# The opening of a fused attention and FFN kernel: w_out in row parts, Q and K in parts behind w3, a new hand-written order

## The chip, the cores and the metric

The kernel runs on one core of a Trainium2 chip. The metric is the device time of one execution in microseconds (us), lower is better. Its engines are named as in the profile: PE (TensorE matmuls; PEld its weight loads), DVE (VectorE), ACT (ScalarE), POOL (GpSimd) and SP (SyncE, here only DMA issues). Each engine takes its instructions in the order of the program and waits on semaphores for the others.

## The reference

Sliding-window causal attention, window 64, over 8 batches, 8 heads, 576 positions, head size 64; then a multiplicative FFN without a nonlinearity on its 4608 rows of 512:

```python
scores = (q @ k.T) / sqrt(64), kept where 0 <= i - j < 64
x = softmax(scores) @ v                 # heads side by side: 4608 x 512
out = (((x @ w1) * (x @ w2)) @ w3) @ w_out   # w1, w2: 512x1024, w3: 1024x1024, w_out: 1024x512
```

Inputs and output are float32; the kernel computes in float16 with float32 sums.

## The kernel before

**Folding.** Since nothing stands between w3 and w_out, the kernel first makes wc = w3 @ w_out (1024 x 512), in eight blocks of 128 rows (fc = 0 to 7). For each block `fold_t` transposes the 128 x 1024 rows of w3 on PE (eight 128 x 128 transposes into one PSUM bank, then one copy to `w3T`), and `fold_mm` multiplies them by w_out, held in `wo16`, and copies the sum from PSUM to `wc_sb`. Blocks 0 to 3 are done in two column halves of 256, blocks 4 to 7 at once, since w_out comes in two column halves.

**Attention.** Each batch has three query segments of 192 positions. `scores(n)` (n = 3 * batch + segment) computes transposed scores of all eight heads into two PSUM tiles; `weigh(d)` (d = 2n, 2n+1, one for each tile, four heads) is the Exp on ACT and the window mask, either two or four selects on POOL or one multiplication by a 0/1 band on DVE; `values(d)` multiplies by V and by ones (giving the row sums), then Ln and Exp(-x) on ACT and a multiplication on DVE write four heads of 192 rows into `xT`. `keep_sums` sends the logarithms of the sums to a buffer for a range check at the end. Q and K arrive as float16 and are transposed on DVE in blocks (`transposes`, L225), a head parity (hh) at a time. In V's tile the columns between the heads are ones (`ones_of`), and `copy_v` copies rows that two key blocks share.

**FFN.** Rows go in nine groups of 512. `ffn_ab(g, fc)` computes a block of 128 columns of x @ w1 and x @ w2 (16 matmuls into two PSUM banks), ACT copies a, DVE multiplies it by b into `ab`. The form `ffn_ab(g, fc, 2, lo, hi)` does two blocks for 256 of the rows, with twice as many matmuls of half the width. `ffn_o(g, t)` multiplies 128 rows by wc (eight matmuls), copies, and `store` sends them out on SP.

**Memory that sets the order.** PSUM is two pools: `ps_a` has two tiles of two banks (scores and values take them in turn), `ps_f` four banks for everything else, handed out in turn: an allocation waits until the fourth one before it has been read. `w3T` has four buffers.

**Order.** The schedule is manual: every engine runs its instructions in the order in which the functions are called. All loads convert float32 to float16 and are issued on POOL, in between POOL's selects. They use eight semaphores in turn, so POOL waits at a load until the eighth load before it has landed. The opening, up to `tick(24)`, which begins with `scores(6)`, is written out by hand; from there on `tick` and a list of due times set the order. It begins: K and Q of batch 0, w_out half 0, w3 rows 0 to 255, the bands, w3 rows 256 to 511, w_out half 1, w3 rows 512 to 767, three blocks of V. Meanwhile `keep_busy(120)` runs matmuls on an identity matrix, whose result is not used, on PE. Then

```python
    scores(0)
    keep_busy(30)
    fold_t(0)
    fold_t(1)
    scores(1)
```

and so on through the fold, with `values(0)` to `values(5)` among its last blocks, then all eight `ffn_ab(0, fc)`, `scores(3)`, `ffn_o(0, 0)`.

Of the kernel before, what the change touches and what calls it, by code (L numbers as in the profile page):

```python
# [15 lines left out]
P = 128  # L16
# [128 lines left out]
def kernel(  # L145
# [25 lines left out]
    EARLY = 2  # L171
# [30 lines left out]
    def load_qk(b, which, *hhs):  # L202
        src = k if which == "k" else q
        r = RUN[b]
        if (which, b) not in t16s:
            t16s[which, b] = sb.tile([P, 2, TI * D], FP16, name=which + "16", bufs=2)
        t = t16s[which, b]
        if not hhs:
            for j in range(NJ):
                nc.gpsimd.dma_start(  # L210
                    out=t[32 * j:32 * j + 32].rearrange("p hh (i n) -> p (hh i) n", n=r * D),
                    in_=src[b, 2 * j:2 * j + 2].rearrange("hh (i p r) d -> p (hh i) (r d)", p=32, r=r))
        for hh in hhs:
            for i in range(2):
                nc.gpsimd.dma_start(
                    out=t[:, hh, i * r * D:(i + 1) * r * D],
                    in_=src[b, hh:H:2, i * 32 * r:(i + 1) * 32 * r].rearrange("j (p r) d -> j p (r d)", p=32, r=r))

    def transposes(b, which, hh):

        dst = kTs if which == "k" else qTs
        r = RUN[b]
        if hh == 0:
            dst[b] = sb.tile([P, 2, S, 2], FP16, name=which + "T")
        nc.vector.transpose(  # L225
            dst[b][:, hh].rearrange("q t c -> q (t c)").bitcast(I32).rearrange("q (i p r) -> q i r p", p=32, r=r),
            t16s[which, b][:, hh].bitcast(I32).rearrange("p (i r e) -> p i r e", r=r, e=32))
# [44 lines left out]
    def scores(n, now=True):  # L272
# [19 lines left out]
        weigh(2 * n)  # L292
        if now:
            weigh(2 * n + 1)

    def weigh(d):

        s_ps = held.pop(d)
        si = d // 2 % 3
        w = s_ps.shape[-1]  # L300

        pt = sb.tile([P, 2, 2, 256], FP16, name="pt", bufs=6)
        nc.scalar.activation(pt[:, :, :, 0:w], s_ps, AF.Exp, bias=-SHIFT, scale=scale)  # L303

        rows = pt.rearrange("k j a n -> k (j a) n")
        if d % 2 == 1 and d < 6 * EARLY:
            band = bands[min(si, 1)]
            nc.vector.tensor_tensor(rows[:, :, 0:w], rows[:, :, 0:w],  # L308
                                    band[:, 0:w].unsqueeze(1).broadcast_to([P, 4, w]), ALU.mult)
        else:  # L310
            select(rows, si)
        probs[d] = pt

    def values(d):
# [7 lines left out]
        o_ps = ps_a.tile([P, 2, 512], FP32, name="a_ps")  # L322
        if jp == 0:
            lns[b, si] = sb.tile([P, NJ, 192], FP32, name="ln_s", bufs=4)
        y = lns[b, si][:, j0:j0 + 2]
        r = sb.tile([P, 2, 192], FP32, name="r")
        x0 = (b * S + q_base) % RING
        xs = xT[:, j0:j0 + 2, x0:x0 + 192]
        if b < SHORT:
# [12 lines left out]
            o, total = (o_ps[:, e, 0:384].rearrange("p (j n) -> p j n", j=2) for e in range(2))  # L342
            nc.scalar.activation(y, total, AF.Ln)
            nc.scalar.activation(r, y, AF.Exp, scale=-1.0)  # L344
            nc.vector.tensor_tensor(xs, o, r, ALU.mult)  # L345
            return
        for jj in range(2):
            first = True
            for a in range(2):
                c0 = 0  # L350
                for bi, (k0, q0, n, _) in enumerate(seg):
# [6 lines left out]
                    c0 += n  # L358
        nc.scalar.activation(y[0:D], o_ps[D:P, :, 0:192], AF.Ln)  # L359
# [23 lines left out]
    def tick(u):  # L383
# [3 lines left out]
        if m == 0 and n < NS:  # L387
            scores(n, now=False)
        if m == 1 and n < NS:
            weigh(2 * n + 1)  # L390
        if m in (1, 2) and 6 < n <= NS:
            values(2 * n - 3 + m)
        for e in late.get(r, []):
            event(b, *e)
# [59 lines left out]
    def load_w12(i, half):  # L454
        cols = slice(half * 512, half * 512 + 512)
# [3 lines left out]
    def load_wo(half):  # L459
        cols = slice(half * 256, half * 256 + 256)  # L460
        nc.gpsimd.dma_start(out=wo16[:, :, cols], in_=moe_w_out[:, cols].rearrange("(e p) m -> p e m", p=P))  # L461

    def load_w3(n):
        fc = 2 * n
        dst = w3a[:, 2 * fc:2 * fc + 4, :].rearrange("p (f a) n -> p f (a n)", f=2) if n < 2 else \
            xT[:, fc - 4:fc - 2, 2 * S:2 * S + DF]
        nc.gpsimd.dma_start(out=dst, in_=moe_w3[fc * P:fc * P + 2 * P].rearrange("(f p) n -> p f n", p=P))

    def fold_t(fc):
# [6 lines left out]
        dve_cp(w3Ts[fc], tp)  # L476

    def fold_mm(fc, c0, c1, cp):
        o_ps = ps_f.tile([P, DM], FP32, name="f_ps")
        for ec in range(8):  # L480
            nc.tensor.matmul(o_ps[:, c0:c1], w3Ts[fc][:, ec, :], wo16[:, ec, c0:c1], start=(ec == 0), stop=(ec == 7))  # L481
        cp(wc_sb[:, fc, c0:c1], o_ps[:, c0:c1])
# [33 lines left out]
    load_qk(0, "k")  # L516
    make_identity(nc, ident16)
    load_qk(0, "q")
    load_wo(0)
    load_w3(0)  # L520
    make_bands()
    load_w3(1)
    load_wo(1)
    load_w3(2)
    load_v(0, 0, 2, 3)
    for i in range(2):
        ones_of(i, nc.vector)
    for which in "kq":
        for hh in range(2):
            transposes(0, which, hh)  # L530
    keep_busy(120)
    scores(0)
    keep_busy(30)
    fold_t(0)
    fold_t(1)
    scores(1)
    load_w3(3)
    load_v(0, 4, 5)
    fold_mm(0, 0, 256, act_cp)
    fold_mm(1, 0, 256, act_cp)  # L540
    fold_t(2)
    fold_t(3)
    scores(2)
    for i in range(2):
        load_w12(i, 0)
    fold_mm(2, 0, 256, act_cp)
    fold_mm(3, 0, 256, act_cp)
    fold_mm(0, 256, DM, act_cp)
    fold_mm(1, 256, DM, act_cp)
    fold_t(4)  # L550
    fold_t(5)
    fold_mm(2, 256, DM, act_cp)
    fold_mm(3, 256, DM, act_cp)
    copy_v(0, 1)
    fold_mm(4, 0, DM, act_cp)
    values(0)
    values(1)
    fold_t(6)
    fold_mm(5, 0, DM, act_cp)
    values(2)  # L560
    values(3)
    copy_v(0, 4)
    fold_t(7)
    fold_mm(6, 0, DM, act_cp)
    values(4)
    values(5)
    fold_mm(7, 0, DM, act_cp)
    for i in range(2):
        load_w12(i, 1)
    load_qk(1, "k")  # L570
    load_qk(1, "q")
    load_v(1, 0, 2, 3, 4, 5)
    for n in range(3):
        keep_sums(n)
    for fc in range(8):
        ffn_ab(0, fc)
        if 2 <= fc < 6:
            transposes(1, "kkqq"[fc - 2], fc % 2)
    load_qk(2, "k")
    load_qk(2, "q")  # L580
    copy_v(1, 1)
    copy_v(1, 4)
    scores(3)
    ffn_o(0, 0)
    store()
    scores(4)
    load_v(2, 0, 2, 3)
    ffn_o(0, 1)
    store()
    scores(5)  # L590
    transposes(2, "k", 0)
    ffn_o(0, 2, act_cp)
    store()
    values(6)
    transposes(2, "k", 1)
    values(7)
    load_v(2, 4, 5)
    ffn_o(0, 3)
    store()
    values(8)  # L600
    transposes(2, "q", 0)
    values(9)
    load_qk(3, "k")
    load_qk(3, "q")
    ffn_ab(1, 0, 2, 0, 256)
    values(10)
    transposes(2, "q", 1)
    ffn_ab(1, 2, 2, 0, 256)
    values(11)
    for n in range(3, 6):  # L610
        keep_sums(n)
# [75 lines left out]
```

## Time and profile before

| | |
|---|---|
| median of 3 runs | 268.28 us (267.68 to 268.68) |
| profiled execution | 268.59 us, of which the span from the first to the last of the program's instructions is 266.8 us |
| PE busy | 254.4 us of the span (95%) |
| DVE, ACT, POOL busy | 169.7, 151.4, 178.7 us |
| granted TensorE clock | 0.997 |
| first `fold_t` on PE | 17.43 us |
| first `ffn_ab` on PE | 39.94 us |
| `scores(6)`, the first step of `tick(24)`, on PE | 72.87 us |

The profile has a page of totals; a timeline and a chain of waits give starts and durations in us from the start of the span. A row such as "17.43 1.07 PE f_ps L474 x16" says: from 17.43 us on, 1.07 us, 16 instructions of line 474 on PE that write the tile f_ps. DMA rows give the bytes that are written (float16) and the median time from issue to landing.

### The profile page before, as it was taken

To read this page: it belongs to the slowest core of one execution; us is meant where nothing else is said; L and a number is where in the kernel's file an instruction comes from. 1 tells how busy PE (TensorE), PEld (TensorE's weight loads), DVE (VectorE), ACT (ScalarE), POOL (GpSimd) and SP (SyncE) were. 2 spreads that over 40 slices of the span, in tenths; PEclk is the share of its full clock that TensorE was granted. 3 is DMA by queue.
4 is the path that set the end of the run, shared out by engine and by line. 5 is a ranking of instruction groups with operands and counts; after the bars stand their busy time and mean duration, and the time that the engine had idled before them with its cause. 6 is when DMAs were issued, how large, how long until landed. Compare 5 with 4: busy or idle time off the path is not lost.

```text
span 266.8 us, 6600 instructions
## 1 busy us (share of the span) xinstructions
PE 254.4 (95%) x2608; PEld 149.7 (56%) x2608; DVE 169.7 (64%) x260; ACT 151.4 (57%) x261; POOL 178.7 (67%) x243
## 2 busy tenths in 40 slices
PE   3979999998999999999999999999999999999992
PEld 3968654445886445545556984545455445444441
DVE  6644454978775675986687567668786565564531
ACT  1037474367656577758874855777498748342300
POOL 7979826679879999999898739687766345005000
PEclk9999999999999999999999999999999999999998
DMA  5999999999999999899999765998540040012013
GB/s 81 170 207 186 189 207 201 131 181 138 149 106 62 131 206 77 61 165 162 62 106 180 102 43 64 202 105 57 99 96 4 7 150 6 0 53 108 0 57 109
DMA packets 75380, 29.45 MB, mean 110 GB/s; under 512 B 62369, under 2 KB 69793, under 8 KB 75345
## 3 DMA queue, kind: packets, MB, share of 16 engines
q0 software_dynamic: 69920, 19.41, 74.9%
q1 hardware_dynamic: 5280, 9.46, 10.0%
q8 instruction: 21, 0.34, 0.6%
q14 instruction: 15, 0.11, 0.2%
q10 hardware_dynamic: 144, 0.13, 0.1%
HBM read 38.80 MB, written 9.44 MB: 181 GB/s over the span
## 4 chain that ended last, share of the span: by engine, by line
PE 87%; DMA 4%; POOL 2%; DVE 2%; ACT 2%; issue 1%; POOLq 0%; DVEq 0%
PE f_ps L417 48%; PE f_ps L435 22%; PE a_ps L353 5%; PE a_ps L286 4%; PE f_ps L481 4%; DMA ab<-in_moe_w_dram 4%; PE a_ps L337 3%; ACT pt L303 1%; PE f_ps L474 1%; POOL q L210 1%; POOL k L210 1%; DVE xT L345 1%; DVE kT L225 1%; POOL ab L461 0%; DVE pt L308 0%
## 5 line engine op out<-in xcount | busy, mean ns | idle before, releaser
L417 PE MATMUL f_ps<-xT,w_sb 128*128 128x512 f16 (+1 forms) x704 | 131.5, 341 | 0.0
L417 PEld LDWEIGHTS <-w_sb 128*128 128x128 f16 x704 | 66.3, 98 | 50.7 <-issue 0.2
L423 DVE TENSOR_TENSOR ab<-f_ps,a_sb 128x512 f16<-128x512 f32 x72 | 49.6, 689 | 33.0 <-PE f_ps L417 31.2
L303 ACT ACTIVATE pt<-a_ps 128x1024 f16<-128x1024 f32 (+1 forms) x48 | 44.5, 953 | 45.4 <-PE a_ps L286 45.4
L258 POOL TENSOR_SCALAR_AFFINE_SELECT pt<-pt 128x1024 f16<-128x1024 f16 (+2 forms) x56 | 46.1, 824 | 30.6 <-ACT pt L303 30.5
L435 PE MATMUL f_ps<-wc_sb,ab 128*128 128x512 f16 (+1 forms) x296 | 66.4, 374 | 0.0
L422 ACT COPY a_sb<-f_ps 128x512 f32<-128x512 f32 x72 | 41.8, 581 | 36.9 <-PE f_ps L417 36.4
L260 POOL TENSOR_SCALAR_AFFINE_SELECT pt<-pt 128x1024 f16<-128x1024 f16 (+2 forms) x56 | 46.5, 831 | 3.9
L435 PEld LDWEIGHTS <-ab 128*128 128x128 f16 x296 | 27.3, 98 | 28.8
L238 POOL DMA_DIRECT2D v<-in_v_dram x40 | 34.0, 860 | 1.0 <-issue 0.4
L362 DVE TENSOR_TENSOR xT<-a_ps,r 64x384 f16<-64x384 f32 x30 | 16.5, 550 | 22.0 <-ACT r L361 22.0
L437 DVE COPY t2k<-f_ps 128x512 f32<-128x512 f32 (+1 forms) x35 | 23.7, 679 | 8.4 <-PE f_ps L435 7.9
L210 POOL DMA_DIRECT2D q<-in_q_dram x32 | 19.7, 621 | 11.8 <-DMA w_sb<-in_moe_w_dram 8.3
L210 POOL DMA_DIRECT2D k<-in_k_dram x32 | 20.1, 634 | 1.6 <-POOLq L671 1.0
L353 PEld LDWEIGHTS <-v 128*128 128x128 f16 x240 | 15.1, 98 | 6.4
L345 DVE TENSOR_TENSOR xT<-a_ps,r 128x384 f16<-128x384 f32 x18 | 10.0, 553 | 13.0 <-ACT r L344 13.0
L359 ACT ACTIVATE ln_s<-a_ps 64x384 f32<-64x384 f32 x30 | 14.6, 487 | 5.8 <-PE a_ps L353 5.0
L353 PE MATMUL a_ps<-pt,v 128*128 128x128 f16 x240 | 17.2, 215 | 0.0
L363 DVE TENSOR_TENSOR xT<-a_ps,r 64x384 f16<-64x384 f32 x30 | 16.8, 561 | 0.4
L286 PEld LDWEIGHTS <-kT 32*128 32x128 f16 x768 | 10.9, 92 | 9.6 <-issue 9.3
L361 ACT ACTIVATE r<-ln_s 128x384 f32<-128x384 f32 x30 | 15.7, 523 | 1.0
L225 DVE STREAM_TRANSPOSE qT<-q 128x576 int32<-128x576 int32 x16 | 14.7, 928 | 1.6 <-DMA q<-in_q_dram 1.6
(44 smaller groups left out, 184.9 us busy)
## 6 DMA issues: line engine op xcount, KB each, us to landing
out_dram<-t2k SPq DMA_DIRECT2D x35, 256.0 KB
k<-in_k_dram POOLq DMA_DIRECT2D x32, 144.0 KB, 6.3
q<-in_q_dram POOLq DMA_DIRECT2D x32, 144.0 KB, 5.8
v<-in_v_dram POOLq DMA_DIRECT2D x32, 128.0 KB, 5.0
w_sb<-in_moe_w_dram POOLq DMA_DIRECT2D x4, 512.0 KB, 9.7
ab<-in_moe_w_out_dram POOLq DMA_DIRECT2D x2, 512.0 KB, 9.5
ab<-in_moe_w_dram POOLq DMA_DIRECT2D x2, 512.0 KB, 9.4
xT<-in_moe_w_dram POOLq DMA_DIRECT2D x2, 512.0 KB, 10.4
```

The source lines that it names most:

```text
L210: nc.gpsimd.dma_start(out=t[32 * j:32 * j + 32].rearrange("p hh (i n) -> p (hh i) n", n=r * D), in_=src[b, 2 * j:2 * j + 2].rearrange("hh ...
L238: nc.gpsimd.dma_start(out=vh[lo:P, c], in_=v[b, :, s0:s0 + P - lo, :].rearrange("h s d -> s h d"))
L258: nc.gpsimd.affine_select(out=sl, in_=sl, pattern=pat, compare_op=ALU.is_ge, fill=0.0, base=off, channel_multiplier=-1)
L260: nc.gpsimd.affine_select(out=sl, in_=sl, pattern=[[-s, m] for s, m in pat], compare_op=ALU.is_ge, fill=0.0, base=63 - off, channel_multip ...
L286: nc.tensor.matmul(s_ps[j // 2][:, j % 2, o0:o0 + m], kT[part, a, k0:k0 + P, c], qT[part, a, q0:q0 + m, c], start=(c == 0), stop=(c == 1), ...
L303: nc.scalar.activation(pt[:, :, :, 0:w], s_ps, AF.Exp, bias=-SHIFT, scale=scale)
L353: nc.tensor.matmul(o_ps[:, jj, o0:o0 + n], v16[:, si * 2 + bi, j0 + jj, a * D:a * D + P], pt[:, jj, a, c0:c0 + n], start=first, stop=(bi = ...
L417: nc.tensor.matmul(d[:, f * n + c0:f * n + c1], w[:, dc, (fc + f) * P:(fc + f + 1) * P], xT[:, dc, xc:xc + c1 - c0], start=first, stop=(dc ...
L422: act_cp(a_sb[:, 0:nf * n], a_ps[:, 0:nf * n])
L423: nc.vector.tensor_tensor(ab[:, fc:fc + nf, lo:hi], b_ps[:, 0:nf * n].rearrange("p (f n) -> p f n", f=nf), a_sb[:, 0:nf * n].rearrange("p ...
L435: nc.tensor.matmul(o_ps[:, 0:c1 - c0], ab[:, fc, t * P:t * P + P], wc_sb[:, fc, c0:c1], start=(fc == 0), stop=(fc == 7))
L437: cp(o_sb[:, c0:c1], o_ps[:, 0:c1 - c0])
```

## The change

- w_out is loaded in two row parts (rows 0 to 511, 512 to 1023) instead of column halves. Every block's fold is then two calls: `fold_mm(fc, 0)` adds four matmuls of 512 columns into a PSUM bank, which is held until `fold_mm(fc, 1)` adds the other four and copies the sum.
- w3 is loaded first, rows 256 to 511 ahead of all, rows 0 to 127 and 128 to 255 one by one, the rest in pairs of blocks. Q and K of batch 0 come behind it, in eight parts: a part is one head parity (hh) and one half of the positions (i, 288 rows) for all four head pairs, where a load before was two heads with all positions. `transposes` takes a part, and halves are transposed one by one.
- `weigh` is told its engine, and `values` is split: `norm` (Ln, Exp, multiplication) is a call of its own. `tick` calls them in the same places as before.
- The call list of the opening is new. The fold begins before attention; group 0 of the FFN is done mostly in the two-block form; V's blocks, the masks' engines, the copies' engines and the loads stand in other places. One `ones_of` moves to POOL. `keep_busy` runs 115 + 20 + 20 matmuls instead of 120 + 30.

The helpers, cut to what changes:

```diff
+    def part_of(b, which, hh, i):
+        r = RUN[b]
+        src = k if which == "k" else q
+        return src[b, hh:H:2, i * 32 * r:(i + 1) * 32 * r].rearrange("j (p r) d -> j p (r d)", p=32, r=r)
+    def load_part(b, which, hh, i):
+        n = RUN[b] * D
+        nc.gpsimd.dma_start(out=t16_of(b, which)[:, hh, i * n:(i + 1) * n], in_=part_of(b, which, hh, i))
-    def transposes(b, which, hh):
+    def transposes(b, which, hh, *i):
...
+        part = slice(i[0], i[0] + 1) if i else slice(0, TI // r)
...
-    def scores(n, now=True):
+    def scores(n):
...
-        weigh(2 * n)
-        if now:
-            weigh(2 * n + 1)
-
-    def weigh(d):
+
+    def weigh(d, engine=nc.gpsimd):
...
-        if d % 2 == 1 and d < 6 * EARLY:
+        if engine is nc.vector:
...
-        o_ps = ps_a.tile([P, 2, 512], FP32, name="a_ps")
+        opened[d] = o_ps = ps_a.tile([P, 2, 512], FP32, name="a_ps")
...
+    def norm(d):
...
+            nc.scalar.activation(y, total, AF.Ln)
+            nc.scalar.activation(r, y, AF.Exp, scale=-1.0)
+            nc.vector.tensor_tensor(xs, o, r, ALU.mult)
...
-    def load_w12(i, half):
-        cols = slice(half * 512, half * 512 + 512)
+    def load_w12(i, c0, c1):
+        cols = slice(c0, c1)
...
-    def load_wo(half):
-        cols = slice(half * 256, half * 256 + 256)
-        nc.gpsimd.dma_start(out=wo16[:, :, cols], in_=moe_w_out[:, cols].rearrange("(e p) m -> p e m", p=P))
+    def load_wo(x):
+        nc.gpsimd.dma_start(out=wo16[:, 4 * x:4 * x + 4, :],
+                            in_=moe_w_out[512 * x:512 * x + 512].rearrange("(e p) m -> p e m", p=P))
...
-    def load_w3(n):
-        fc = 2 * n
+    def load_w3(fc, n):
...
-    def fold_t(fc):
+    def fold_t(fc, cp):
...
-        dve_cp(w3Ts[fc], tp)
-    def fold_mm(fc, c0, c1, cp):
-        o_ps = ps_f.tile([P, DM], FP32, name="f_ps")
-        for ec in range(8):
-            nc.tensor.matmul(o_ps[:, c0:c1], w3Ts[fc][:, ec, :], wo16[:, ec, c0:c1], start=(ec == 0), stop=(ec == 7))
-        cp(wc_sb[:, fc, c0:c1], o_ps[:, c0:c1])
+        cp(w3Ts[fc], tp)
+    sums = {}
+    def fold_mm(fc, x, cp):
+        if x == 0:
+            sums[fc] = ps_f.tile([P, DM], FP32, name="f_ps")
+        o_ps = sums[fc]
+        for ec in range(4 * x, 4 * x + 4):
+            nc.tensor.matmul(o_ps, w3Ts[fc][:, ec, :], wo16[:, ec, :], start=(ec == 0), stop=(ec == 7))
+        if x == 1:
+            cp(wc_sb[:, fc, :], o_ps)
```

The new call list up to `tick(24)` (several calls on a line here; `act_cp`, `dve_cp` name the copying engine):

```diff
+    load_w3(2, 2); make_identity(nc, ident16); keep_busy(115); load_w3(0, 1); fold_t(2, act_cp); make_bands();
+    keep_busy(20); load_wo(0); fold_t(3, dve_cp); keep_busy(20); load_part(0, 'k', 1, 0); load_part(0, 'q', 1, 0);
+    load_part(0, 'q', 0, 0); fold_t(0, dve_cp); load_wo(1); fold_mm(2, 0, dve_cp); fold_mm(3, 0, dve_cp);
+    load_w3(1, 1); fold_mm(2, 1, act_cp); load_part(0, 'k', 0, 0); load_w3(4, 2); load_part(0, 'q', 1, 1);
+    ones_of(1, nc.vector); load_part(0, 'k', 1, 1); ones_of(0, nc.gpsimd); transposes(0, 'q', 0, 0);
+    load_part(0, 'k', 0, 1); load_v(0, 3); fold_mm(0, 0, act_cp); fold_t(1, act_cp); transposes(0, 'q', 1, 0);
+    transposes(0, 'k', 0, 0); transposes(0, 'k', 1, 0); fold_mm(0, 1, act_cp); load_part(0, 'q', 0, 1);
+    load_v(0, 0); load_v(0, 2); fold_mm(3, 1, act_cp); transposes(0, 'q', 1, 1); fold_mm(1, 0, dve_cp);
+    load_w3(6, 2); load_w12(0, 0, 512); scores(0); transposes(0, 'k', 1, 1); weigh(0, nc.gpsimd); load_v(0, 4);
+    fold_t(5, act_cp); fold_t(4, dve_cp); transposes(0, 'k', 0, 1); transposes(0, 'q', 0, 1); fold_mm(1, 1, dve_cp);
+    fold_mm(5, 0, act_cp); load_w12(1, 0, 512); fold_mm(4, 0, dve_cp); load_v(0, 5); copy_v(0, 1);
+    weigh(1, nc.vector); scores(1); weigh(3, nc.gpsimd); fold_mm(4, 1, dve_cp); weigh(2, nc.vector); values(0);
+    values(1); norm(0); fold_t(7, dve_cp); norm(1); values(2); fold_mm(5, 1, dve_cp); load_w12(0, 512, 1024);
+    norm(2); values(3); keep_sums(0); copy_v(0, 4); fold_mm(7, 0, act_cp); load_w12(1, 512, 1024); norm(3);
+    fold_t(6, act_cp); fold_mm(7, 1, dve_cp); scores(2); load_qk(1, 'k'); load_v(1, 4); fold_mm(6, 0, act_cp);
+    weigh(4, nc.vector); load_qk(1, 'q'); weigh(5, nc.vector); ffn_ab(0, 0, 2, 0, 256); fold_mm(6, 1, dve_cp);
+    values(5); values(4); norm(4); norm(5); ffn_ab(0, 2, 2, 0, 256); ffn_ab(0, 4, 2, 0, 256); load_v(2, 0);
+    ffn_ab(0, 0, 2, 256, 512); transposes(1, 'k', 0); load_qk(2, 'k'); ffn_ab(0, 4, 2, 256, 512);
+    transposes(1, 'k', 1); transposes(1, 'q', 1); transposes(1, 'q', 0); ffn_ab(0, 6); ffn_ab(0, 7); load_v(1, 2);
+    load_v(1, 0); load_qk(2, 'q'); ffn_ab(0, 2, 2, 256, 512); transposes(2, 'k', 1); keep_sums(1); copy_v(1, 1);
+    load_v(1, 3); load_v(2, 2); scores(3); weigh(7, nc.gpsimd); weigh(6, nc.vector); ffn_o(0, 0, act_cp);
+    transposes(2, 'k', 0); scores(4); ffn_o(0, 1, dve_cp); load_v(1, 5); weigh(9, nc.gpsimd); store();
+    weigh(8, nc.vector); scores(5); weigh(10, nc.gpsimd); ffn_o(0, 2, dve_cp); weigh(11, nc.vector); values(6);
+    norm(6); keep_sums(2); load_v(2, 4); values(7); store(); norm(7); copy_v(1, 4); ffn_o(0, 3, act_cp); values(8);
+    transposes(2, 'q', 1); values(9); norm(8); norm(9); keep_sums(3); ffn_ab(1, 0, 2, 0, 256);
+    transposes(2, 'q', 0); store(); load_v(2, 5); values(10); keep_sums(4); values(11); load_qk(3, 'k');
+    load_qk(3, 'q'); norm(10); norm(11); keep_sums(5); ffn_ab(1, 2, 2, 0, 256); load_v(2, 3); U0 = 24;
+    ffn_ab(1, 4, 2, 0, 256)
```

More of the change, by code (lines that the diff above doesn't have):

```diff
@@ L561 @@
+    norm(2)
     values(3)
+    keep_sums(0)
     copy_v(0, 4)
-    fold_t(7)
-    fold_mm(6, 0, DM, act_cp)
-    values(4)
[L566 to L580, printed above, removed]
```

262 lines of the change are left out of this document (169 added, 93 removed).

## The prediction

> **What bounds the kernel now.** I read the page first: PE is busy for 254.4 of 266.8 us and carries 87% of the chain of waits, so time can come only from PE's few idle stretches or from matmuls taken away. The chain in order of time shows where they lie (start, duration, what):
>
> ```profile
> PE 254.4 (95%) x2608; PEld 149.7 (56%) x2608; DVE 169.7 (64%) x260; ACT 151.4 (57%) x261; POOL 178.7 (67%) x243
> 7.51 9.87 DMA ab<-in_moe_w_dram
> ...
> 17.43 1.07 PE f_ps L474 x16
> ...
> 27.06 3.47 PE f_ps L481 x24
> 30.53 0.82 PE a_ps L337 x32
> ...
> 40.10 13.93 PE f_ps L417 x64
> 54.03 0.46 PE a_ps L286 x31
> ...
> 72.94 0.46 PE a_ps L286 x32
> ```
>
> Until 17.43 PE does little but warm itself; it waits there for the first rows of w3 (issued at 7.51, landed at 17.38). After that PE has work in every piece; the timeline shows idle gaps of 0.26 and 0.78 us and a few tenths more up to `scores(6)` at 72.9, and none that matters later. The code is the same from `tick(24)` on, so the change is worth what it moves the start of `scores(6)`.
>
> The loads come next. Three windows of the DMA view (3 to 12, 13 to 23, 43 to 46 us), and the issue row of V's first block, issued at 13.27:
>
> ```profile
> DMA packets 1591, 1.40 MB, mean 156 GB/s; under 512 B 128, under 2 KB 1591, under 8 KB 1591
> DMA packets 2002, 2.09 MB, mean 209 GB/s; under 512 B 69, under 2 KB 1307, under 8 KB 2000
> DMA packets 614, 0.61 MB, mean 202 GB/s; under 512 B 95, under 2 KB 612, under 8 KB 614
> v<-in_v_dram POOLq DMA_DIRECT2D x1, 128.0 KB, 13.7
> ```
>
> The DMA engines are busy all the time, but bring only 156 GB/s before 12 us; Q and K of batch 1, in the same shape, came at 202. V's block landed at 13.27 + 13.7 = 27.0, as the fourteenth load.
>
> **The change, part by part.** *PE's early start.* One w3 load (0.72 us of POOL) instead of four K loads (2.44) stands before the identity, so PE starts 1.7 us earlier, at 2.86. The 120 warming matmuls took 8.95 us; five fewer at the late spacing (30 in 1.85, 0.06 each) leave 8.65, so the fold begins at 11.5. Three transposes of 0.5 (sixteen took 1.07), twice 20 warming matmuls (1.2) and two row-part folds of 0.87 (eight 512-wide matmuls take 1.73) bring PE to 17.1. Next, `fold_mm(2, 1)` needs w_out's second part, the seventh load: 2.28 MB in, 1.40 of it by 12.0, the rest at 209 GB/s by 16.2, and a load lands some 1.4 us after its bytes are due by this count (w3's first rows, 2.23 MB: 16.0 against 17.38). So 17.6, a wait of 0.5.
>
> *Q and K behind w3.* From there PE has six more row-part folds, three transposes and `scores(0)` (0.5), 8.1 us with the first, and stands before `fold_mm(4, 0)` at 25.7. That needs a PSUM bank of `ps_f`, freed by DVE's copy of block 1, and the copy is queued on DVE behind the transposes of the last part of Q, the fifteenth load. `scores(1)`, right behind it on PE, needs that part too, so the wait is there with or without the bank. The fifteen loads hold the same bytes as the first fourteen of before: eight 144 KB pieces of Q and K, 2.5 MB of weights, one block of V, 3.93 MB. By the count they land at 12.0 + 2.53 MB / 209 + 1.4 to 2.0 = 25.5 to 26.1; by V's row at 27.0, with more V behind it in the same stretch. I take 26.0. DVE then needs half a transpose (0.6; the whole takes 1.13 to 1.21) and the copy (0.68), so `fold_mm(4, 0)` starts at 27.4: PE waits 1.7.
>
> *What PE still has to do from there to `scores(6)`*, from rows: 7 row-part folds 6.1, two transposes 1.0, `scores` 1 and 2 1.15, `values` 0 to 5 2.9 (0.82 + 1.01 + 1.08), group 0 of the FFN 14.35 (six two-block calls at 1.81, where three in a row took 5.34, and two whole ones at 1.74; 0.4 more than the 13.93 of before), `scores` 3 to 5 1.65, four outputs 7.3, `values` 6 to 11 3.3, three two-block calls of group 1 5.55: 43.3 us. Before, at 27.4, 44.3 us were left. So by then six microseconds of earlier start have shrunk to a lead of 1.0, because the loads, not PE, set the pace of the opening.
>
> *New waits behind it.* These rows price them:
>
> ```profile
> 19.11 1.94 ACT L303 ACTIVATE pt<-a_ps 128x1024 f16<-128x1024 f32 x2 [2.63 <-PE a_ps L286]
> 32.13 0.56 DVE L345 TENSOR_TENSOR xT<-a_ps,r 128x384 f16<-128x384 f32 x1 [3.55 <-ACT r L344]
> 46.11 1.21 DVE L225 STREAM_TRANSPOSE kT<-k 128x576 int32<-128x576 int32 x1
> ```
>
> (1) `values(0)` takes the PSUM tile of `scores(1)` whose Exp is the second of two: 2.6 us after `scores(1)` begins (18.43 to 21.05), while PE has 0.57 + 0.87 to do: 1.15. (2) `values(2)` takes the tile of `values(0)`, free 2.2 us after that began (30.46 to 32.69: Ln, Exp, multiplication); PE has 1.5: 0.75. (3) Late in group 0, DVE's queue has three whole transposes of batch 1 in a row ahead of the multiplication for block 6, whose bank the last two-block call needs for its second half: from PE's end of `ffn_ab(0, 0, 2, 256, 512)` DVE has 0.36 + 3 x 0.69 + 4 x 1.21 = 7.3 to that bank, PE 1.81 + 2 x 1.74 + 0.9 = 6.2: 1.1. (4) About 0.3 at `scores(5)`, behind two Exps, as before. Together 3.3, where before had 1.2. One gain is in here: `values(9)` loses the 0.78 in which it waited for a DVE transpose.
>
> *Hidden.* POOL's 128x3072 memset of ones (2.6 us on DVE; on POOL 0.33 for 256 columns, so 3 to 4) delays the issue of the last parts to some 18.5, well ahead of 26. `weigh(0)` and `weigh(3)` on POOL stand behind loads that wait for their semaphore: done near 26 and 32.5, needed at 31 and 34.6. The second halves of w1 and w2 are issued near 33, with four loads outstanding, and land by 43, needed at 44.3; a late one would cost PE its lateness. The stores and sums on SP move among themselves; nothing waits for them. The copies of w3T on ACT (1.0 for 1024 columns, by the 0.97 of an Exp) and `norm` as a call of its own change nothing on PE. Holding sums in PSUM costs nothing beyond the bank above.
>
> *Sum.* 27.4 + 43.3 + 3.3 = 74.0, against 72.9, nearly all of it copied to the end: +1.0. The profiled execution took 268.59 (span 266.8 and 1.8 around it), 0.3 above the median of 268.28. So 269.6 in its terms, 269.3 in the median's.
>
> **Rivals.** *Faster: the slow first 12 us belong to what was loaded then.* If w3 and w_out come at 209 GB/s from 3 us on, the fifteenth load lands 2.3 us earlier, near 23.7, and PE's own 16.9 + 8.1 sets `fold_mm(4, 0)` to 25.1: 71.7, 1.2 us before 72.9, a time of 267.1 (266.3 if a part of the new waits closes too, 267.8 if only half the loss is gone). For it: the same shape reached 202 GB/s later, so shape alone is not slow. Against it: the loss is the only record of a first 12 us, and it went on after DVE's two memsets had ended (7.44), which the change takes away from there (9 to 12 us: 166 GB/s). The Trainium skill ("SBUF — State Buffer", Who interferes with whom) says that a DVE instruction with at most one SBUF input outside the two-port modes does not hold up GpSimd; by it the memsets are not the cause, and these rows agree.
>
> *Slower: the parts use fewer DMA engines.* A part's source has 4 head pairs as its slowest dimension, where every load from POOL before begins with 32 or more rows. If it is cut over only four of the sixteen engines, one part takes four times 0.73 (147 KB at 202 GB/s), 2.9 us. Taken in turns the engines stay evenly loaded, but the last four parts land together near 26 instead of one after another; DVE then does two more half transposes and a copy (1.9) before the copy that PE waits for: 271.2. If it were always the same four, eight parts hold them for 23.4 us instead of 5.8, and the time is about 287. It decides if K's last two parts land after 24.1 (26.0 less two half transposes and a copy). No row speaks for or against. This is a rule of the Trainium skill ("DMA: Bandwidth & Descriptors", Why a DMA increments its semaphore by 16 and not by 1): the number of engines is the largest up to 16 that divides the slowest dimensions of both sides; it names an exception for some direct copies, which then use all 16. No run here shows which holds.
>
> That the change does not do what it says is no rival: the orders on the engines are those of the call list. That the row parts and held sums matter by themselves I exclude: the eight folds' matmuls cost PE 13.8 to 14.0 either way.
>
> **How the numbers follow.** My case 0.47 (268.6 to 270.4, the load at 25.3 to 27.0), the faster rival 0.27, the slower one 0.20 in turns and 0.03 on the same engines, 0.03 for a wait that I missed. Over 0.5% (1.34 us), about what a measurement of this kernel can tell from no change, mean under 266.9 or over 269.6. Faster: half of the rival and a little of my case, 0.17. Slower: a third of mine, nearly all of the other rival and the rest, 0.38. Within: 0.45. The range leaves out the 287 and the outer tails: 266.5 to 271.4.
>
> **What would show it.** Right: first transpose on PE at 11 to 12; `fold_mm(4, 0)` near 27.4, waiting for DVE, DVE for a Q load that landed near 26; gaps of about 1 before `values(0)`, `values(2)` and the last two-block call of group 0; `scores(6)` near 74. Wrong: the Q load before 24.5 or after 28, a part that lands 3 us after its neighbour, or new gaps after 54 us.

## The result, and the profile after

The changed kernel takes 269.78 us (median of 4 executions, 269.42 to 270.24) against 268.19 us before: a ratio of 1.0060, 95% interval 1.0036 to 1.0085. Run again beside later experiments it took 269.62 us (12 executions, 268.59 to 271.68) against 268.22: 1.0049 (1.0025 to 1.0073). The forecast was 269.3, in a range of 266.5 to 271.4. The profiled execution took 270.24 us, its span 268.5 us.

The page's line of totals, first of the changed kernel:

```profile
PE 255.6 (95%) x2629; PEld 152.0 (57%) x2629; DVE 166.4 (62%) x264; ACT 152.8 (57%) x257; POOL 180.2 (67%) x243
```

PE is as much the bound as before. The chain in order of time (start, duration, what) shows the difference of the opening: where before PE's own pieces stood from 17 us on, two loads and a memset on POOL now carry most of the first 29 us.

```profile
7.00 7.72 DMA k<-in_k_dram
15.69 2.67 POOL v L531
19.85 8.98 DMA q<-in_q_dram
30.28 1.94 ACT pt L306 x2
...
43.42 12.29 PE f_ps L432 x96
```

PE's timeline shows the same (start, duration, line, tiles, count; in brackets the idle time before it and what ended it). L499 is `fold_mm`, L292 `scores`, L334 `values`:

```profile
18.75 1.89 PE L499 MATMUL f_ps<-ab,w3T 128*128 128x512 f16 x8 [1.10 <-DMA ab<-in_moe_w_out_dram]
...
23.61 0.53 PE L292 MATMUL a_ps<-qT,kT 32*128 32x128 f16 x32
...
27.53 1.04 PE L499 MATMUL f_ps<-ab,w3T 128*128 128x512 f16 x4 [0.54 <-DVE w3T L490]
29.60 0.64 PE L292 MATMUL a_ps<-qT,kT 32*128 32x128 f16 x32 [1.03 <-DVE qT L231]
...
31.45 0.54 PE L334 MATMUL a_ps<-pt,v 128*64 128x128 f16 x16 [0.24 <-ACT pt L306]
32.27 0.54 PE L334 MATMUL a_ps<-pt,v 128*64 128x128 f16 x16 [0.28 <-ACT pt L306]
...
33.80 0.64 PE L334 MATMUL a_ps<-pt,v 128*64 128x128 f16 x16 [0.44 <-DVE xT L370]
```

`scores(1)`, which began at 18.43 before, waits for the last part of Q. That part is issued late: POOL, which may have eight loads under way, stood 2.02 us until the part of K issued at 7.00 had landed, issued the next part and then made the memset. And it comes slowly, as the DMA view says. Its windows 3 to 12, 13 to 23 and 23 to 29 us, and the issue row of that part (issued at 19.85, landed 9.0 later):

```profile
DMA packets 1800, 1.39 MB, mean 154 GB/s; under 512 B 840, under 2 KB 1416, under 8 KB 1800
DMA packets 2964, 1.88 MB, mean 188 GB/s; under 512 B 1596, under 2 KB 2579, under 8 KB 2963
DMA packets 4188, 0.90 MB, mean 151 GB/s; under 512 B 3774, under 2 KB 4139, under 8 KB 4187
q<-in_q_dram POOLq DMA_DIRECT2D x1, 144.0 KB, 9.0
```

The 13 to 23 us window brings 188 GB/s instead of 209, in packets of which over half have 4 bytes. The packet records of the first 31 us hold 3353 packets of 4 bytes, against 301 before. In the 23 to 29 us window 2846 packets are V's, of 128 bytes: its first three blocks are issued around the last part of Q, at 18.94, 20.54 and 21.45.

From there to `scores(6)` the table of busy time reads (window, its length, PE busy, instructions, granted clock, DMA share, GB/s):

```profile
27.50:73.25 45.75, 43.69 (x588) 1.00 1.37 177
```

`scores(6)` starts at 73.25, 0.38 later than before. But this is not all of the difference. In the common part behind it PE stops once more:

```profile
81.72 1.03 PE L432 MATMUL f_ps<-xT,w_sb 128*128 128x256 f16 x8 [1.05 <-DVE ab L438]
```

and DVE, which PE waits for, had been standing in `copy_v(2, 4)`:

```profile
80.31 0.64 DVE L248 COPY v<-v 64x512 f16<-64x512 f16 x1 [5.55 <-DMA v<-in_v_dram]
```

The block of V that this copies from is `load_v(2, 3)`, which the new list issues behind `load_qk(3, 'k')` and `load_qk(3, 'q')`; it was issued at 73.26 and landed at 80.28. From `scores(8)` on, PE runs 1.58 us later than before, to its last matmul.

### The profile page after: what moved, and what is told of

It is laid out like the page before. It is cut to its first block, busy times and chain, and to the rows that moved or that the text cites. A ratio compares the mean times of both kernels' runs of the same rounds, so it can differ in the third digit from the quotient of the medians.

```text
span 268.5 us, 6623 instructions
## 1 busy us (share of the span) xinstructions
PE 255.6 (95%) x2629; PEld 152.0 (57%) x2629; DVE 166.4 (62%) x264; ACT 152.8 (57%) x257; POOL 180.2 (67%) x243
## 4 chain that ended last, share of the span: by engine, by line
PE 85%; DMA 6%; POOL 3%; ACT 1%; issue 1%; DVE 1%; DVEq 0%; POOLq 0%
PE f_ps L432 47%; PE f_ps L450 24%; PE a_ps L292 5%; PE a_ps L346 5%; DMA q<-in_q_dram 3%; PE a_ps L334 3%; DMA k<-in_k_dram 3%; PE f_ps L499 2%; POOL v L531 1%; ACT pt L306 1%; POOL k L222 0%; POOL band L266 0%; POOL band L264 0%; POOL v L244 0%; POOL ab L475 0%
## 5 line engine op out<-in xcount | busy, mean ns | idle before, releaser
L432 PEld LDWEIGHTS <-w_sb 128*128 128x128 f16 x752 | 71.0, 98 | 47.4 <-issue 1.2
L264 POOL TENSOR_SCALAR_AFFINE_SELECT pt<-pt 128x1024 f16<-128x1024 f16 (+2 forms) x55 | 44.5, 809 | 31.1 <-ACT pt L306 31.0
L266 POOL TENSOR_SCALAR_AFFINE_SELECT pt<-pt 128x1024 f16<-128x1024 f16 (+2 forms) x55 | 45.5, 827 | 3.8
L452 DVE COPY t2k<-f_ps 128x512 f32<-128x512 f32 (+1 forms) x34 | 23.0, 679 | 9.3 <-PE f_ps L450 8.7
L206 POOL DMA_DIRECT2D q<-in_q_dram x28 | 17.8, 651 | 5.0 <-DMA w_sb<-in_moe_w_dram 3.9
L206 POOL DMA_DIRECT2D k<-in_k_dram x28 | 17.7, 648 | 1.0 <-issue 1.0
L231 DVE STREAM_TRANSPOSE qT<-q 128x576 int32<-128x576 int32 (+1 forms) x18 | 14.9, 842 | 4.5 <-DMA q<-in_q_dram 4.5
L499 PE MATMUL f_ps<-ab,w3T 128*128 128x512 f16 x64 | 15.8, 380 | 1.6 <-DMA ab<-in_moe_w_out_dram 1.1
L346 PE MATMUL a_ps<-pt,v 128*128 128x128 f16 x240 | 17.2, 215 | 0.0
L292 PEld LDWEIGHTS <-kT 32*128 32x128 f16 x768 | 10.9, 92 | 10.5 <-issue 10.5
```

Source lines behind the costliest of these rows:

```text
L206: nc.gpsimd.dma_start(out=t[32 * j:32 * j + 32].rearrange("p hh (i n) -> p (hh i) n", n=r * D), in_=src[b, 2 * j:2 * j + 2].rearrange("hh ...
L264: nc.gpsimd.affine_select(out=sl, in_=sl, pattern=pat, compare_op=ALU.is_ge, fill=0.0, base=off, channel_multiplier=-1)
L266: nc.gpsimd.affine_select(out=sl, in_=sl, pattern=[[-s, m] for s, m in pat], compare_op=ALU.is_ge, fill=0.0, base=63 - off, channel_multip ...
L292: nc.tensor.matmul(s_ps[j // 2][:, j % 2, o0:o0 + m], kT[part, a, k0:k0 + P, c], qT[part, a, q0:q0 + m, c], start=(c == 0), stop=(c == 1), ...
L346: nc.tensor.matmul(o_ps[:, jj, o0:o0 + n], v16[:, si * 2 + bi, j0 + jj, a * D:a * D + P], pt[:, jj, a, c0:c0 + n], start=first, stop=(bi = ...
L432: nc.tensor.matmul(d[:, f * n + c0:f * n + c1], w[:, dc, (fc + f) * P:(fc + f + 1) * P], xT[:, dc, xc:xc + c1 - c0], start=first, stop=(dc ...
```

## The experiments

All start from the changed kernel unless said otherwise. Two measures are used: the time, and the offset of PE's instructions against the kernel before, taken from PE's rows in the profiled executions at the calls of `scores`.

**The late V block.** `a_v23` issues it earlier:

```diff
+    load_v(2, 3)
     load_qk(3, 'k')
     load_qk(3, 'q')
...
-    load_v(2, 3)
```

> The changed kernel with one call moved: V's third block of batch 2 (load_v(2, 3)) is issued just before load_qk(3, 'k') instead of behind load_qk(3, 'q') and four other calls. Theory: the 1.2 us that the changed kernel loses after scores(6) is the wait of copy_v(2, 4) for this block (DVE waited 5.55 us for it, landing at 80.28). Then the step near 81.7 on PE goes, scores(6) stays at 73.2 to 73.3, everything behind it runs 0.3 to 0.5 us later than in the kernel before instead of 1.6, and the time is 268.5 to 268.8 us, 1.0 to 1.3 under the changed kernel. Rival: DVE is late there anyway (the wait only shows on the V load because it came last), so PE loses most of the 1.2 us to DVE's queue: 269.3 to 269.8.

Measured: 269.52 us (12 executions, 268.45 to 271.2), ratio to before 1.0046 (1.0024 to 1.0067); profiled execution 268.80. PE's offset is 0.85 us at `scores(6)` and still 0.85 at the last `scores`: the step is gone, as the theory said. The median did not fall as it said, but lies where the rival had it. So the changed kernel itself was run again:

> The changed kernel itself, unedited, timed again beside the others of this call, because the kernel with V's third block of batch 2 issued earlier scattered from 268.45 to 271.2 us in twelve executions (median 269.52), while its profiled execution (268.80) was 1.44 us under the profiled one of the changed kernel. Theory: the late V block costs 1.2 us in most executions, and the landings of the parts in the opening vary by 1 to 2 us between executions in both kernels: this one then has a median of 270 to 270.7 over twelve executions, above the four seen so far (269.78), with the same scatter. Rival: the V block costs nothing in the median and its kernel is simply as slow as this one: 269.4 to 269.9.

Measured: 269.62 us, as the rival had it. In its profiled execution (269.44) the last part of Q landed at 29.24 and the offset at `scores(6)` is 0.79, yet the V block costs only 0.25 us (offset 1.04 from `scores(8)` on), though DVE waited for it as well:

```profile
79.68 0.71 DVE L248 COPY v<-v 64x512 f16<-64x512 f16 x1 [4.51 <-DMA v<-in_v_dram]
```

The block landed 0.6 us sooner and PE came 0.4 us later, and both come off the wait. The three profiled executions with the late issue have a step of 1.20, 0.25 and 0.65 us there (the third is `b_pairs`, below), the six with the earlier issue have none. The wait is real and its price in these executions is 0.25 to 1.2 us; the medians, of times that scatter over 3 us, do not show it.

**The form of the parts.** `d_parts_before` takes the kernel before and changes only how K and Q of batch 0 are cut:

```diff
-    load_qk(0, "k")
+    for hh in range(2):
+        for i in range(2):
+            load_part(0, "k", hh, i)
...
-    load_qk(0, "q")
+    for hh in range(2):
+        for i in range(2):
+            load_part(0, "q", hh, i)
```

> The kernel before with one thing of the change alone: K and Q of batch 0, still loaded first, come as eight parts (one head parity, half of the positions, all four head pairs, 4 x 32 rows) instead of eight loads of one head pair each, same bytes. Theory: a part is cut over four of the sixteen DMA engines and the other twelve get 32 packets of 4 bytes each. Then 8 x 384 = 3072 packets of 4 bytes come on top of the 286 of the kernel before, the first K part lands at 6.4 to 7 us instead of 4.84 (2.5 us on four engines against 0.7 on sixteen), several parts land together, and the last at 12 to 13.5 us (12.09 before); PE, which waits at 17.43 for w3's first rows, gets them up to 1.5 us later: 268.4 to 269.9. Rival: the parts are on all sixteen engines: first landing at 4.8, no extra packets, 268.2 to 268.6.

Measured: 272.19 us, ratio 1.0141 (1.0114 to 1.0167), 4.0 us slower: the theory's mechanism, at more than twice the price that it gave. The DMA view from 3 to 8 us, when nothing but K and Q is under way, and the issue rows of the first part of K (issued at 1.43) and of the last two of Q:

```profile
DMA packets 1385, 0.26 MB, mean 53 GB/s; under 512 B 1161, under 2 KB 1385, under 8 KB 1385
k<-in_k_dram POOLq DMA_DIRECT2D x1, 144.0 KB, 6.2
q<-in_q_dram POOLq DMA_DIRECT2D x2, 144.0 KB, 8.8
```

The same of the kernel before (its first load of K is issued at 1.49):

```profile
DMA packets 742, 0.77 MB, mean 153 GB/s; under 512 B 77, under 2 KB 742, under 8 KB 742
k<-in_k_dram POOLq DMA_DIRECT2D x1, 144.0 KB, 3.4
q<-in_q_dram POOLq DMA_DIRECT2D x2, 144.0 KB, 5.9
```

A third of the bytes, and fifteen times the packets under 512 bytes. The packet records give the sizes: a load of 144 KB is 128 packets of 1152 bytes in either form, and each part brings 384 of 4 bytes more, twelve times 32 (3329 of 4 bytes in the first 31 us, 3028 more than before, for eight parts). That fits four engines with 32 packets of data each and twelve with 32 empty ones; on which engine a packet was, the records do not tell. A data packet took 0.107 us in the median in either kernel, so the packets were not slower, there were fewer at a time: from 3 to 6 us 97 of them, 3.5 engines' worth at 0.107 us, against 363 before, and 38 GB/s, though four parts had been issued by 4.39. From 9.5 to 12.5 us, with more parts under way, it was 167 GB/s. So the parts were neither spread over all sixteen engines from the start nor always on the same four.

The last part of Q lands at 15.84 instead of 12.09, 3.75 later. PE feels it through POOL's eight loads: w3's first rows are issued at 9.82 instead of 7.51, when the second part of K has landed, and land at 20.79 instead of 17.38. PE's offset is 3.6 us from `scores(1)` on: the opening's loss goes to the end undiminished.

`b_pairs` keeps the changed kernel's order and takes the parts away, at the price of more loads: each part becomes two loads of one head pair and both head parities.

```diff
+    def load_pair(b, which, jp, i):
...
+        for j in (2 * jp, 2 * jp + 1):
+            nc.gpsimd.dma_start(
+                out=t16_of(b, which)[32 * j:32 * j + 32, :, i * r * D:(i + 1) * r * D],
+                in_=src[b, 2 * j:2 * j + 2, i * 32 * r:(i + 1) * 32 * r].rearrange("hh (p r) d -> p hh (r d)", p=32, r=r))
```

> The changed kernel with each of the eight part loads of Q and K of batch 0 replaced by two loads of one head pair each (both head parities, one half of the positions, 32 rows first in the source), same bytes at the same eight places of the list. Theory: a part is cut over only four of the sixteen DMA engines, so it takes 2.5 us alone, and the twelve others get 4-byte packets instead. Then the 3000 extra packets of 4 bytes go, the loads land at even distances, the last Q part near 26 to 27 instead of 28.83, scores(1) starts at 27.5 to 28.5 instead of 29.60, and the time is 1.0 to 2.3 us under the changed kernel: 267.5 to 268.8. Rival 1: the parts are on all engines already and the opening is late for want of bandwidth: no change, 269.5 to 270.0. Rival 2: twice as many issues (eight more at about 0.7 us on POOL, and the limit of eight loads under way) cost as much as the engines bring: last Q part at 28 to 30, 269.5 to 271.

Measured: 272.61 us, ratio 1.0145 (1.0107 to 1.0183): worse than rival 2. The 4-byte packets are gone (385 in the first 31 us) and loads of 72 KB land 0.4 us apart, but POOL now stands before the eleventh load, until the third has landed, and again before the last of Q (POOL's timeline):

```profile
14.71 0.55 POOL L489 DMA_DIRECT2D ab<-in_moe_w_dram  x1 [3.75 <-DMA ab<-in_moe_w_out_dram]
...
26.05 0.54 POOL L228 DMA_DIRECT2D q<-in_q_dram  x1 [1.30 <-DVE qT L239]
```

The second line is a wait that no theory had: the last loads of Q waited for DVE's transposes of pieces that came before. They then share the DMA engines with V: from 25 to 30 us these bring 96 GB/s at a mean share of 1.12, with 1981 packets of 128 bytes among 2243, and the last piece of Q lands at 30.03.

```profile
DMA packets 2243, 0.48 MB, mean 96 GB/s; under 512 B 2062, under 2 KB 2242, under 8 KB 2242
```

DVE's timeline shows a second cost, which has nothing to do with the DMA engines:

```profile
25.05 0.70 DVE L239 STREAM_TRANSPOSE qT<-q 128x288 int32<-128x288 int32 x1 [5.55 <-DMA q<-in_q_dram]
...
30.12 0.70 DVE L239 STREAM_TRANSPOSE qT<-q 128x288 int32<-128x288 int32 x1 [2.48 <-DMA q<-in_q_dram]
```

A piece holds both head parities, a transpose takes one parity of all four pairs. The first line is `transposes(0, 'q', 1, 0)`: its pieces had landed by 16.52, yet it starts when a piece of the other half has landed, at 24.96. Why the program waits there is not shown. The second is `transposes(0, 'q', 1, 1)`, which needs Q's last piece here, where in the changed kernel it needed a part that landed at 25.68; three more transposes and a copy stand behind it. So `scores(1)` starts 2.97 us after Q's last landing instead of 0.77. `b_pairs` changes more than the number of engines, and does not tell what sixteen loads cost by themselves.

`c_both` adds the earlier V block, `f_bands` moves the bands (POOL, 2.7 us) behind the issues as well:

```diff
     fold_t(2, act_cp)
-    make_bands()
...
     load_pair(0, 'k', 0, 1)
+    make_bands()
     ones_of(0, nc.gpsimd)
```

> Both edits at once: V's third block of batch 2 issued before load_qk(3, 'k'), and the eight parts as sixteen loads of one head pair each. Theory: the two causes are in different stretches (before 30 us and near 80 us) and add: 2.0 to 3.5 us under the changed kernel, 266.3 to 267.8, which would beat the kernel before (268.2) by 0.4 to 1.9. Rival: PE, once earlier, meets another late load or the DVE queue behind scores(6), so that only the larger of the two gains is left: 267.8 to 268.8.

> As the kernel with both edits, and make_bands() moved from ahead of load_wo(0) to just before the memset of ones on POOL, so that w_out's first part is issued some 2.5 us earlier. Theory: in the changed kernel the DMA engines stood nearly idle at 7.5 to 8.5 us (41 and 84 GB/s), because POOL built the bands; without the gap all later loads land 0.5 to 1 us earlier, w_out's second part too, and PE gains 0.3 to 0.8 us over the kernel with both edits. Rival: the bands' work on POOL only moves in front of the last parts, whose issue then is late (POOL, not the DMA engines, sets the landing of the last Q part): same or up to 1 us slower than the kernel with both edits.

Measured: 271.32 us (1.0118, 1.0091 to 1.0146) and 272.36 us (1.0141, 1.0116 to 1.0166). Both theories fell, and the rival of `c_both` too, since both kernels have the pieces of `b_pairs` and its waits: in `c_both` the last piece of Q lands at 28.82, as the last part did in the changed kernel (28.83), and `scores(1)` starts at 31.80 instead of 29.60. `c_both` does confirm that the step near 80 us goes (offset 2.58 throughout). `f_bands` went as its rival said. Still it answers a question of the prediction: with the bands out of the way the DMA engines brought 200 to 213 GB/s in every 2 us window from 7 to 19 us, and w_out's first part landed at 10.58 instead of 11.97. The slow first 12 us are thus not a matter of the time since the start. After that POOL built bands and ones from 17.2 to 22.5 us, the last four loads of Q and K were issued behind them, and PE stood:

```profile
27.66 0.61 PE L300 MATMUL a_ps<-qT,kT 32*128 32x128 f16 x24 [4.22 <-DVE kT L239]
```

**Whole loads behind w3.** These runs suggest a list with loads on all sixteen engines, no more of them than before, and POOL's own work behind the issues. `g_whole` does that with the forms that the kernel before has:

```diff
     load_w3(2, 2); make_identity(nc, ident16)
+    ones_of(1, nc.vector)
...
-    make_bands()
...
+    load_qk(0, 'k')
     fold_t(0, dve_cp); load_wo(1); load_w3(1, 1)
+    make_bands()
...
+    load_qk(0, 'q')
     load_w3(4, 2); ones_of(0, nc.gpsimd); load_v(0, 3); load_v(0, 0); load_v(0, 2)
```

The eight `load_part` go. K is transposed whole, Q by halves; `fold_mm(3, 1)` becomes the first fold behind `fold_mm(2, 1)`, `scores(1)` stands ahead of `fold_mm(4, 0)`, some copies change between ACT and DVE, and `load_v(2, 3)` is issued ahead of `load_qk(3, 'k')`.

> The changed kernel with the opening's loads in the form of the kernel before at the same count: K of batch 0 in four loads of one head pair (all positions, 32 rows first) behind w_out's first part, Q in four behind w3's rows 128 to 255, both ahead of w3's rows 512 to 767; the bands built behind those issues, the memset of ones for DVE at the very start; transposes of K whole, of Q by halves; fold_mm(3, 1) and scores(1) earlier in PE's list; V's third block of batch 2 issued before load_qk(3, 'k'). Bytes are the same. Theory: the changed kernel's opening is late because parts keep only four engines busy and halves in other forms run into the limit of eight loads under way; with eight whole loads the DMA engines bring about 200 GB/s from 5 us on, the last Q load lands near 21 instead of 28.83, scores(1) starts at 25.5 to 26.5 instead of 29.60, scores(6) at 70 to 71 instead of 73.25, and the time is 265.3 to 266.8 us, below the kernel before (268.2). Rival 1: the weights, V and w1, w2 behind Q set the pace (they hold 4.4 MB to the last piece of w2, which landed at 44.06): PE's lead is given back before the FFN and only 0.3 to 1 us is left: 267.3 to 268.2. Rival 2: PE waits elsewhere in the new order (w_out's second part later than 18): 268.2 or more.

Measured: 267.22 us (12 executions, 266.44 to 268.04), ratio 0.9959 (0.9943 to 0.9974): 1.0 us faster than before, 2.4 under the changed kernel on the same chip. The mechanism held, the price was a little high: between the theory and its rival 1. Windows 8 to 12 and 13 to 23 us of the DMA view, and the row of the last load of Q, issued at 12.41, landed at 21.05:

```profile
DMA packets 807, 0.82 MB, mean 205 GB/s; under 512 B 48, under 2 KB 807, under 8 KB 807
DMA packets 2285, 2.00 MB, mean 200 GB/s; under 512 B 875, under 2 KB 1901, under 8 KB 2285
q<-in_q_dram POOLq DMA_DIRECT2D x1, 144.0 KB, 8.6
```

`scores(1)` starts at 26.1, `scores(6)` at 71.12, and the offset stays at -1.75 to the end.

`g_parts` puts only the form back into it:

```diff
-    load_qk(0, 'k')
+    load_part(0, 'k', 1, 0); load_part(0, 'k', 1, 1); load_part(0, 'k', 0, 0); load_part(0, 'k', 0, 1)
...
-    load_qk(0, 'q')
+    load_part(0, 'q', 0, 0); load_part(0, 'q', 1, 0); load_part(0, 'q', 1, 1); load_part(0, 'q', 0, 1)
```

> The kernel g_whole with one thing put back: K and Q of batch 0 come as the changed kernel's eight parts (4 x 32 rows, all head pairs) instead of eight whole loads of one head pair, at the same places of the same list. Theory: the form itself costs the opening, since a part feeds only part of the sixteen DMA engines (in the kernel before with parts the last piece of Q landed 3.75 us later and the time rose by 4.0). Then the last Q part lands at 22.5 to 24.5 instead of 21.05, about 3000 packets of 4 bytes come back, and the time is 1 to 3 us above g_whole's 267.2: 268.2 to 270.2. Rival: the gain of g_whole came from its order (Q and K ahead of w3's rows 512 to 767, bands behind the issues), and the weights keep the other engines busy meanwhile: 267.0 to 267.7.

Measured: 269.23 us (8 executions, 268.3 to 270.19), ratio to before 1.0038 (1.0019 to 1.0058) where `g_whole` had 0.9959 (0.9943 to 0.9974). The last part of Q lands at 23.66, 2.6 later, and `scores(6)` starts at 73.22, 2.1 later. One edit, and the changed kernel's place beside the kernel before is back: the form of the parts costs 2.0 us here, and in this list it makes the difference between faster and slower than before. Part of it comes through POOL again: the third part of Q is issued at 15.57, after a wait of 3.10 for a part of K, where the last load of Q in `g_whole` was issued at 12.41.

`g_swap` is `g_whole` with PE's list mended at the longest wait that its timeline showed:

```diff
-    values(2); fold_mm(5, 1, dve_cp)
+    fold_mm(5, 1, dve_cp); values(2)
...
-    values(3); keep_sums(0); copy_v(0, 4); fold_mm(7, 0, act_cp)
+    fold_mm(7, 0, act_cp); values(3); keep_sums(0); copy_v(0, 4)
```

> The kernel g_whole with two pairs of calls exchanged: fold_mm(5, 1) ahead of values(2), and fold_mm(7, 0) ahead of values(3). In g_whole PE waited 1.30 us before values(2) for DVE's xT, with fold_mm(5, 1) (0.87 us) ready behind it. Theory: what PE waits in the opening moves everything behind it, to the end: the 0.87 us fit into the wait, scores(6) comes 0.7 to 0.9 us earlier than 71.12, and the time is 266.3 to 266.6. Rival: values(3) or scores(2) meets the wait that values(2) loses (their PSUM tiles come free from the same chain of Ln, Exp and multiplication): 266.8 to 267.3.

Measured: 266.12 us (6 executions, 265.82 to 267.07), ratio 0.9927 (0.9909 to 0.9945), the fastest of all. The wait in `g_whole` and what became of it in `g_swap`:

```profile
31.67 0.64 PE L334 MATMUL a_ps<-pt,v 128*64 128x128 f16 x16 [1.30 <-DVE xT L370]
```

```profile
31.77 0.64 PE L334 MATMUL a_ps<-pt,v 128*64 128x128 f16 x16 [0.41 <-DVE xT L370]
```

The 0.89 went into `fold_mm(5, 1)`, as expected, and `scores(2)` starts 0.74 earlier (35.32 instead of 36.06). But `scores(2)` then loses 0.38 within itself, waiting for the PSUM tile that DVE's multiplication frees, which is what the rival had said:

```profile
35.32 0.23 PE L292 MATMUL a_ps<-qT,kT 32*128 32x128 f16 x2
35.70 0.63 PE L292 MATMUL a_ps<-qT,kT 32*128 32x128 f16 x30
```

So `scores(6)` is 0.36 earlier in these two executions, half of what the theory forecast. Their spans differ by 1.3 us, and 0.9 of that lies behind PE's last matmul (4.5 us to the end in `g_swap`, 5.4 in `g_whole`). The medians are of different chips; the ratios to before differ by 0.0032, some 0.9 us, and their intervals touch. That the exchange is worth more than 0.36 us is not shown.

## Why the prediction was right, step by step

The direction and the size were right: 269.3 forecast, 269.6 to 269.8 measured. The path was right too: the last part of Q sets the pace of the opening, and what PE loses there is copied to the end. Several steps were not right, and their errors went in opposite directions; that they left only 0.3 to 0.5 us is partly luck.

**"The code is the same from `tick(24)` on, so the change is worth what it moves the start of `scores(6)`."** In all ten profiled executions beside the one of the kernel before, PE's offset is the same from `scores(8)` to the last `scores`, within 0.02 us, however large it is (-2.1 to +4.7). But the code being the same does not make its inputs the same: the new list issues the V block for `copy_v(2, 4)` in the last calls before `tick(24)`, and this wait behind `scores(6)` cost 0.25 to 1.2 us. The prediction had "new gaps after 54 us" among the signs that it is wrong, and costed no load behind `scores(6)`.

**PE's early start.** The fold begins at 12.18 instead of 11.5 (PE starts at 3.02, and the warming matmuls last 9.2 us, not 8.65). `fold_mm(2, 1)` begins at 18.75 instead of 17.6, waiting 1.10 for w_out's second part, and PE reaches `fold_mm(4, 0)` at 26.99 instead of 25.7.

**"I take 26.0" for the fifteenth load.** It landed at 28.83. This is the term that was most mis-sized. The count took 209 GB/s from 12 us on; the window 13 to 23 us brought 188, which is worth about 1.1 us. The rest falls behind 23 us, where V's packets of 128 bytes stand among the part's and the rate is 151; and the part was issued at 19.85, not at some 18.5. How the rest divides between the two is not shown. The slower rival's mechanism was true, and so was its condition: K's last two parts landed at 26.23 and 26.60, after 24.1. The Trainium skill ("DMA: Bandwidth & Descriptors", Why a DMA increments its semaphore by 16 and not by 1) gives the number of engines as the largest up to 16 that divides the slowest dimensions of both sides, which is 4 here. The 12 x 32 packets of 4 bytes of each part agree with it, and the exception that it names did not apply. The prediction held this rival at 0.23 since, as it says, no row spoke for or against; `d_parts_before` and `g_parts` are that row.

**The rival's price, 1.9 us, was too high, and wait (1) for the same reason.** It let DVE do two half transposes and the copy of block 1 before the bank that `fold_mm(4, 0)` needs came free. The section on the kernel before says that an allocation of `ps_f` waits until the fourth one before it has been read. It does not: `fold_mm(4, 0)` starts at 27.53, and the copy of block 1, the fourth allocation before it, stands on DVE at 29.40:

```profile
26.26 0.70 DVE L231 STREAM_TRANSPOSE kT<-k 128x288 int32<-128x288 int32 x1
26.80 0.67 DVE L490 COPY w3T<-f_ps 128x1024 f16<-128x1024 f16 x1
27.40 0.67 DVE L231 STREAM_TRANSPOSE kT<-k 128x288 int32<-128x288 int32 x1
28.85 0.69 DVE L231 STREAM_TRANSPOSE qT<-q 128x288 int32<-128x288 int32 x1 [0.78 <-DMA q<-in_q_dram]
29.40 0.67 DVE L501 CAST wc_sb<-f_ps 128x512 f16<-128x512 f32 x1
```

So it took another bank, one that was free. In the same way `values(0)` took a tile of `ps_a` at 31.45, before the second Exp of `scores(1)` ended at 32.22, whose tile the prediction gave it. The forecast of 27.4 for `fold_mm(4, 0)` was met for another reason: its operand, block 4's copy to `w3T`, stood on DVE behind the transpose of a K part that landed at 26.23.

**43.3 us of work and 3.3 of waits to `scores(6)`.** The work was nearly right: 43.69 us busy in the 45.75 from there. The waits are 2.06 in place of 3.3: (1) and (2) come to 0.24 + 0.28 + 0.44 instead of 1.9, (3) does not exist, (4) is there as before but stands inside the row of `scores(5)` (0.90 us long instead of 0.64) and so counts as work, and 1.03 before `scores(1)` was not in the list. So 27.5 + 43.7 + 2.06 makes the 73.25, against the 74.0 forecast: Q 2.8 us later than taken had cost about one, the waits of the list gave back more, and the V block, not in the sum, added 1.20 in this execution and 0.25 in the second.

**The faster rival** had its premise confirmed and not its gain: w3, and w_out and K behind it in loads of full width (`f_bands`, `g_whole`), do come at 191 to 213 GB/s from 5 to 19 us. In the changed kernel the parts and the bands ahead of w_out took that away. Freed of both, with its list shifted a little and the V block earlier, the opening gives 267.2 (`g_whole`). The rival's 267.1 is close to that, but by a coincidence: it was forecast for the changed kernel's own list, with the parts.

Open remains how the executions of one kernel come to scatter over 3 us in the changed opening (268.45 to 271.68 in 24 executions with and without the earlier V block) where the kernel before has 1.7 (267.37 to 269.08 in 23); only single executions have a profile.

## What to carry to other kernels

Before a load is cut differently, look at the slowest dimension of both its sides: a cut that keeps the number of loads and bytes can leave a load on a quarter of the DMA engines, as the 4-byte packets and the rate of 38 GB/s suggest here. When the number of loads under way is limited, a slow load also holds back the issue of those behind it. Before pieces are cut another way, look at which of them each reader then needs: in `b_pairs` that cost 2.2 us. And where a hand-written opening hands over to code that stays the same, check not only when the first engine arrives there but also which of its inputs were issued last.

## What the runs showed of the hardware that was not expected

- A load from POOL whose source begins with 4 head pairs left 384 packets of 4 bytes, besides its 128 of data; with nothing else under way such loads brought 53 GB/s from 3 to 8 us (`d_parts_before`) where those with 32 rows first brought 153.
- A block of V comes in 1024 packets of 128 bytes, which take 0.032 us each in the median: where they stand, the rate falls to 151 GB/s (23 to 29 us in the changed kernel) with the engines busy.
- The granted clock of TensorE fell to 0.50 (26 to 30 us) in `f_bands`, where PE waited 1.30 and then 4.22 us with 0.29 of work between, and to 0.51 (22 to 24 us) in `b_pairs` after one wait of 2.65 us; two waits of 1.65 us in `c_both` left it at 1.00 in the 5 us windows around them. The Trainium skill ("TensorE: Matmul & The Clock Gate", What's actually happening) puts the fall to half after at least one idle window of about 3.4 us. Here a wait of 2.65 us was enough.
- From the end of PE's last matmul to the end of the span it took between 4.4 us (`f_bands`) and 5.4 us (`g_whole`), with the same code there: up to 1 us of the difference between two executions lies behind PE's last work.
